# Two attention decodes on one core: B's last two wo rows in four transfers instead of eight, a new order of the last loads, and A's result in one store

## The chip, the cores and the metric

The kernel runs on one core of a Trainium2 chip. The metric is device time in microseconds (us) for one execution. Before the change three runs took 825.72 to 825.73 us, median 825.73 us.

## The reference

Two independent attention decodes, A and B, each with one query token, 32 heads of 128 and its own cache; the two results stand side by side in a [1, 1, 1024] output.

```python
q = (x @ wq)                                   # x: [1, 512], wq: [512, 4096], 32 heads of 128
scores = einsum("bhqd,bhkd->bhqk", q, k) * 128 ** -0.5
p = softmax(scores)
o = einsum("bhqk,bhkd->bhqd", p, v)
result = o.reshape(1, 1, 4096) @ wo            # wo: [4096, 512]
```

A attends to all 16384 keys of each head. B attends to the last 4096 keys. All data are bf16. A's K and V caches (128 MiB each) and the part of B's that is read (32 MiB each) are streamed once through the core; each side's `wq` and `wo` are 4 MiB.

## The kernel before

**The main stream.** The work is cut into 20 steps, 16 of A (two heads each) and 4 of B (eight heads each); step 19, the last, is B's. A step loads an 8 MiB K tile `kt` and an 8 MiB V tile `vt`, all through SyncE's DMA queue (SP), in an order written out by hand (`tc.manual_schedule()`, L382). VectorE (DVE) multiplies K by the query (`scores_prod`, L213) and sums over the head dimension by a tree of adds (`scores_tree`, L219, L223). ScalarE (ACT) makes the exponentials (`soft`), and TensorE (PE) multiplies them by V (`pv`, L277) one step later.

**The tail.** After the last step's scores no K is left to work on, and what remains is short: the last softmax, the last `pv`, the normalisation of both sides, and two products with `wo`:

- `wide_a` (L336): A's output times A's `wo`, 32 matmuls of 512 columns; `finish_a` (L349) adds the four groups of rows, copies the row to SBUF on ACT (L353) and stores it (L355), in three stores on ACT's queue.
- `spread_o(B)` (L325) makes `OpB`, 32 columns of 128 partitions: column r holds the elements 32p + r of B's attention output. A further copy `Ox` (L331) brings the columns 30 and 31 of partitions 64 to 127 down to partitions 0 to 63.
- `project_b` (L357): 30 terms `OpB[:, r]` by `wo_t[:, r, :]`, and two more columns from the tile `extra`, in all one accumulation in a PSUM bank. Each term is four matmuls, one for each quarter of the 512 output columns. Terms 0 to 24 come first, then those of `extra`, then 25 to 29. DVE copies the sum (L374), and four stores, two on SP and two on ACT, write it out (L376).

**Where B's wo lies.** Partition p holds the rows 32p to 32p + 31 of `wo`. Its rows r = 0 to 29 come in four pieces over all 128 partitions, by `load_wo` (L142): piece 0 is rows 0 to 15 (2048 KB), piece 1 rows 16 to 24 (1152 KB), piece 2 rows 25 to 28 (512 KB), piece 3 row 29 (128 KB). The two rows that are left of each partition, 30 and 31 (2 KB together), go by `load_extra` (L147) into 64 partitions of the tile `free`, the lower half of the 128 partitions beside the upper half. This takes eight transfers, written -1 to -8 in the order; each has eight partitions (every fourth one in a group of 32), 4 KB for each partition, 32 KB in all. `wo_order` (L381) is the order in which SP issues them:

```python
wo_order = (-1, -2, -3, 0, -4, -5, -6, 1, -7, -8, 2, 3)
```

**What sets the order.** SP issues its transfers strictly in program order, and waits at the head of its queue. Besides waits for data, the framework gives each transfer one of eight semaphores, in turn, over SP's and ACT's transfers together, in the order in which its planner places them; a transfer waits until the one that had its semaphore before, eight places back, has landed. In the program before, the places at the end are: A's `wo`, -1, -2, -3, piece 0, the three stores of A's row, -4, -5, -6, piece 1, -7, -8, piece 2, piece 3, and the four stores of B's row. A store on ACT's queue can thus hold up a load on SP's. The planner places by its own forecast of time, so where the store of A's row comes among the loads is not written in the kernel.

Of the kernel before, what the change touches and what calls it, by code (L numbers as in the profile page):

```python
# [10 lines left out]
BF16 = mybir.dt.bfloat16  # L11
P = 128
# [4 lines left out]
HQ, DH = 32, 128  # L17
# [8 lines left out]
def kernel(  # L26
# [14 lines left out]
    nc = tc.nc  # L41
# [4 lines left out]
    DN = A_wo.shape[1]  # L46
# [4 lines left out]
    singles = ctx.enter_context(tc.tile_pool(name="singles", bufs=1))  # L51
# [8 lines left out]
    QR = P // NG  # L60

    def kslot(name):
        return kring.tile([P, 2 * CH, DH], BF16, tag="kring", name=name)

    def vslot(name):
        return vring.tile([P, 2 * CH, DH], BF16, tag="vring", name=name)
# [7 lines left out]
    A, B = _Side(), _Side()  # L74
    for k, (s, n, x, wq, wo, nh) in enumerate(((A, "A", A_x, A_wq, A_wo, 2), (B, "B", B_x, B_wq, B_wo, 4))):
# [7 lines left out]
        s.cs = singles.tile([P, HQ // nh], F32, tag=f"cs{n}", name=f"cs{n}")  # L83
        s.mask = singles.tile([P, nh], F32, tag=f"mask{n}", name=f"mask{n}")
        s.acc = ps_o.tile([P, 512], F32, tag=f"acc{n}", name=f"acc{n}")
    Ox = singles.tile([P // 2, 2], BF16, tag="Ox", name="Ox")
    o_banks = [ps_o.tile([P, 512], F32, tag=f"o{k}", name=f"o{k}") for k in range(2)]
    sm_banks = [ps_o.tile([P, 512], F32, tag=f"sm{k}", name=f"sm{k}") for k in range(2)]

# [18 lines left out]
    def flat(t):  # L108
        return t.rearrange("p l d -> p (l d)")
# [15 lines left out]
    def new_k(T):  # L125
        K[T] = kslot("kt")

    def load_k(T, parts=(0, 1)):
        load(T, A_k_cache, B_k_cache, K[T], parts)
# [5 lines left out]
    def load_wq(s):  # L135
        nc.sync.dma_start(  # L136
            out=s.wq_t.rearrange("p (c f) -> p c f", c=KC), in_=s.wq.rearrange("(p c) f -> p c f", c=KC)
        )
# [3 lines left out]
        nc.sync.dma_start(out=s.wo_t[:, r : r + n, :], in_=src[:, r : r + n, :])  # L142

    NX = 2
    PX = P // 2

    def load_extra(s, k):  # L147
        x, b = divmod(k, 4)
        src = s.wo.rearrange("(u p r) f -> p u (r f)", u=2, r=HQ)
        at = slice(32 * x + b, 32 * (x + 1), 4)  # L150
        nc.sync.dma_start(out=extra[at, :, :], in_=src[at, :, (HQ - NX) * DN : HQ * DN])

    def make_masks(s):
# [16 lines left out]
    def clear_x(s, t):  # L170
        s.xb = t[:, 0 : s.nh * KC * P].rearrange("p (h c m) -> p h c m", h=s.nh, c=KC)
        nc.vector.memset(s.xb, 0.0)
# [125 lines left out]
    def pick_blocks(o, src, n, weight):  # L298
        nc.vector.tensor_scalar(out=o, in0=src[:, 0:n], scalar1=weight[:, 0:1], scalar2=None, op0=ALU.mult)
        for j in range(1, 4):  # L300
            nc.vector.scalar_tensor_tensor(
                out=o, in0=src[:, j * n : (j + 1) * n], scalar=weight[:, j : j + 1], in1=o, op0=ALU.mult, op1=ALU.add
            )
# [21 lines left out]
    def spread_o(s):  # L325
        nc.tensor.matmul(s.ps[:, 1 : 1 + P], lhsT=fours[:, :], rhs=s.own[:, :], start=True, stop=True)
        t = small.tile([P, HQ], F32, tag="t", name="t", bufs=1)
        pick_blocks(t[:, :], s.ps[:, 1 : 1 + P], HQ, s.rq)
        nc.vector.tensor_copy(s.Op[:, :], t[:, :])
        if s is B:  # L330
            nc.vector.tensor_copy(Ox[:, :], t[PX:P, HQ - NX : HQ])  # L331

    def o_column(s, r):
        return s.Op[:, r : r + 1].broadcast_to([P, QR])
# [14 lines left out]
    def finish_a():  # L349
        ps = sm_banks[0]  # L350
        nc.tensor.matmul(ps[0:1, :], lhsT=first, rhs=A.wide[:, :], start=True, stop=True)  # L351
        row = one.tile([1, DN], BF16, tag="sc", name="row_a")
        nc.scalar.copy(row[:, :], ps[0:1, :])  # L353
        for a, b in ((0, DN // 2), (DN // 2, 3 * DN // 4), (3 * DN // 4, DN)):
            nc.scalar.dma_start(out=out[0, :, a:b], in_=row[:, a:b])  # L355

    def project_b():  # L357
        w = DN // NG
        ps = sm_banks[1]
        terms = [(o_column(B, r), B.wo_t[:, r, :]) for r in range(HQ - NX)]  # L360
        more = [
            ((Ox[:, j : j + 1] if u else B.Op[0:PX, HQ - NX + j : HQ - NX + j + 1]).broadcast_to([PX, QR]),
             extra[:, u, j * DN : (j + 1) * DN])
            for u in range(2) for j in range(NX)
        ]
        terms = terms[0:25] + more + terms[25:]
        for k, (o, wo) in enumerate(terms):
            for g in range(NG):
                nc.tensor.matmul(  # L369
                    ps[QR * g : QR * (g + 1), 0:w], lhsT=o, rhs=wo[:, g * w : (g + 1) * w],  # L370
                    start=(k == 0), stop=(k == len(terms) - 1),
                )
        rows = one.tile([P, w], BF16, tag="Mr", name="rows_b")
        nc.vector.tensor_copy(rows[:, :], ps[:, 0:w])  # L374
        for g in range(NG):
            (nc.sync if g % 2 else nc.scalar).dma_start(  # L376
                out=out[0, :, DN + g * w : DN + (g + 1) * w], in_=rows[QR * g : QR * g + 1, :]
            )

    wo_pieces = ((0, 16), (16, 9), (25, 4), (29, 1))  # L380
    wo_order = (-1, -2, -3, 0, -4, -5, -6, 1, -7, -8, 2, 3)  # L381
    with tc.manual_schedule():  # L382
        xrow = one.tile([2, D], BF16, tag="pm", name="xrow")
        for s in (B, A):
            nc.scalar.dma_start(out=xrow[s.k : s.k + 1, :], in_=s.x[0, :, :])
        scratch = kslot("scratch")
        new_k(0)
        wqt = vslot("wqt")
        for k, s in enumerate((B, A)):
            s.wq_t = flat(wqt[:, k * CH : (k + 1) * CH, :])  # L390
        load_wq(B)
        load_k(0, (0,))
        load_wq(A)
        load_k(0, (1,))
        make_identity(nc, identf[:, :])
        nc.vector.tensor_copy(two_b[:, :], identf[0:2, 0:2])
        nc.vector.memset(ones[:, :], 1.0)
        nc.vector.tensor_reduce(
            out=quad[:, :], in_=identf[:, :].rearrange("p (m c) -> p c m", c=4), axis=AX.X, op=ALU.add
        )  # L400
        block = small.tile([P, P // 4], F32, tag="block", name="block", bufs=1)
        nc.vector.tensor_reduce(
            out=block[:, :], in_=identf[:, :].rearrange("p (m c) -> p m c", c=4), axis=AX.X, op=ALU.add
        )
        nc.vector.tensor_copy(
            fours[:, :].rearrange("p (m c) -> p m c", c=4), block[:, :].unsqueeze(2).broadcast_to([P, P // 4, 4])
        )
        clear_x(B, flat(scratch[:, :, :]))
        clear_x(A, one.tile([P, 2 * KC * P], BF16, tag="o4", name="xbA")[:, :])
        for o in o_banks:  # L410
            nc.vector.memset(o[:, :], 0.0)
        for s in (B, A):
            make_masks(s)
        turn_x(xrow)
        for s in (B, A):
            spread_x(s)
        project_q(B)
        project_q(A)
        new_k(1)
        load_k(1)  # L420
        for T in range(NT):
            if T >= 1:
                if T + 1 < NT:
                    new_k(T + 1)
                    load_k(T + 1)
                else:
                    load_v(T, kslot("vlast"))
            scores_prod(T, 0)
            if T >= 1:
                max_all(T - 1)  # L430
                soft(T - 1)
            if steps[T][0] is A:
                scores_prod(T, 1)
            else:
                scores_tree(T, 0, CH)
            if T >= 1:
                for u in range(tiles[T - 1].s.units):
                    pv(T - 1, u)
                for u in range(tiles[T - 1].s.units):
                    fold(T - 1, u)  # L440
            if T + 1 < NT:
                load_v(T, vslot("vt"))
            else:
                wot = vslot("wot")
                for k, s in enumerate((A, B)):
                    s.wo_t = flat(wot[:, k * CH : (k + 1) * CH, :]).rearrange("p (r f) -> p r f", r=HQ)
                load_wo(A, 0, HQ)
            if steps[T][0] is A:
                scores_tree(T, 0, 2 * CH)
            else:  # L450
                scores_prod(T, 1)
                scores_tree(T, CH, 2 * CH)
            tile_max(T)
        free = flat(kslot("free")[:, :, :])
        extra = free[0:PX, 0 : 2 * NX * DN].rearrange("p (u n) -> p u n", u=2)
        for k in wo_order:
            if k < 0:
                load_extra(B, -1 - k)
            else:
                load_wo(B, *wo_pieces[k])  # L460
        max_all(NT - 1)
        soft(NT - 1)
        normalize(A)
        own_o(A)
        pv(NT - 1, 0)
        spread_o(A)
        pv(NT - 1, 1)
        normalize(B)
        for u in range(2):
            fold(NT - 1, u)  # L470
        own_o(B)
        wide_a()
        spread_o(B)
        finish_a()
        project_b()


# [28 lines left out]
```

## Time and profile before

| | |
|---|---|
| median of three runs | 825.73 us |
| time of the profiled execution | 825.79 us |
| span of its trace, from the first to the last instruction | 823.7 us |
| busy: DVE, PE, ACT | 755.6, 178.3, 61.4 us |
| read from memory | 352.32 MB, mean 428 GB/s |
| the last K tile's scores end (DVE, L229) | 796.3 us |

Times of the trace count from the start of the span; 2.09 us of the profiled execution's time lie outside it. In a timeline each row has the start, the length from the first instruction's start to the last one's end, the engine, the line, and in brackets the idle time before it and what ended it. "SPq" and "ACTq" are the instructions that issue transfers. A row "wot<-in_B_wo_dram" is a piece of B's `wo`, "free<-in_B_wo_dram" one of the transfers -1 to -8. A transfer's landing shows where an engine that waited for it starts.

### The profile page before, as it was taken

Reading aid. Unit: us, or ns where it says so; the run is one execution under the profiler, and the core shown is the slowest. Engines: PE = TensorE matmul, PEld = TensorE weight load, DVE = VectorE, ACT = ScalarE, POOL = GpSimd, SP = SyncE. Lnnn points to the kernel's source line nnn. Section 1 sums busy time; section 2 is a strip of 40 time slices with the busy share of each in tenths; the row PEclk is TensorE's granted clock in tenths of the full one; section 3 lists DMA queues with packets and bytes.
Section 4 is the critical chain, followed back from the end, with each engine's and each line's share of the span. In section 5 each row is a group of like instructions: output and inputs, shape, how many; then the busy total and the mean of one; then the engine's idle time right before and its main releaser. Section 6 shows DMA issues by size and latency. Waiting matters only on the chain.

```text
span 823.7 us, 3859 instructions
## 1 busy us (share of the span) xinstructions
PE 178.3 (22%) x1614; PEld 59.4 (7%) x1614; DVE 755.6 (92%) x269; ACT 61.4 (7%) x165; POOL 0.7 (0%) x6
## 2 busy tenths in 40 slices
PE   3402212203030302230311213020403020302145
PEld 1100000101010000000000001000100000000012
DVE  2899899999999999999999999998999998999972
ACT  0102000001010000200000001000100000000021
POOL 0000000000000000000000000000000000000000
PEclk9765656566565656555656565565556565656568
DMA  9999999999999999999999999999999999999996
GB/s 384 438 433 437 446 423 446 437 426 439 424 446 423 427 442 442 415 448 426 439 426 437 430 436 421 446 440 420 453 420 446 426 440 426 446 417 450 417 430 252
DMA packets 8146, 352.56 MB, mean 428 GB/s; under 512 B 959, under 2 KB 1090, under 8 KB 1346
## 3 DMA queue, kind: packets, MB, share of 16 engines
q1 hardware_dynamic: 8116, 352.33, 99.1%
q8 instruction: 12, 0.20, 0.1%
q14 instruction: 4, 0.03, 0.0%
q10 hardware_dynamic: 14, 0.00, 0.0%
HBM read 352.32 MB, written 0.00 MB: 428 GB/s over the span
## 4 chain that ended last, share of the span: by engine, by line
DMA 50%; DVE 47%; PE 2%; issue 0%; ACT 0%; SPq 0%; DVEq 0%; ACTq 0%
DMA kt<-in_A_k_cache_dram 44%; DVE kt L213 22%; DVE kt L219 21%; DMA kt<-in_B_k_cache_dram 5%; DVE sc L223 3%; PE o L277 1%; DMA wot<-in_B_wo_dram 0%; DMA out_dram<-row_a 0%; DVE Mr L243 0%; DVE M L239 0%; PE wide L340 0%; PE accB L293 0%; ACT pm L265 0%; PE sm L351 0%; SPq L136 0%
## 5 line engine op out<-in xcount | busy, mean ns | idle before, releaser
L219 DVE TENSOR_TENSOR kt<-kt 128x16384 bf16<-128x16384 bf16 (+3 forms) x96 | 335.1, 3491 | 3.2
L213 DVE TENSOR_TENSOR kt<-kt,qA 128x16384 bf16<-128x16384 bf16 x32 | 277.8, 8682 | 23.3 <-DMA kt<-in_A_k_cache_dram 23.3
L277 PE MATMUL o<-vt,pm 128*8 128x512 bf16 (+1 forms) x1216 | 108.4, 532 | 182.8 <-DMA vt<-in_A_v_cache_dram 163.0
L213 DVE TENSOR_TENSOR kt<-kt,qB 128x16384 bf16<-128x16384 bf16 x8 | 69.5, 8685 | 13.9 <-DMA kt<-in_B_k_cache_dram 13.9
L277 PEld LDWEIGHTS <-pm 128*8 128x8 bf16 (+1 forms) x1280 | 38.5, 111 | 250.2 <-issue 200.8
L233 PE MATMUL sm<-identf,m 128*1 128x128 f32 (+1 forms) x20 | 7.5, 373 | 225.0 <-DVE m L229 225.0
L223 DVE TENSOR_REDUCE sc<-kt 128x256 f32<-128x2048 bf16 (+1 forms) x24 | 46.3, 1931 | 2.1
L246 PE MATMUL sm<-identf,Mr 1*128 1x1 f32 (+1 forms) x20 | 5.2, 262 | 190.1 <-DVE Mr L243 190.1
L252 ACT ACTIVATE bias<-sm 128x1 f32<-128x1 f32 (+1 forms) x20 | 3.4, 171 | 448.7 <-PE sm L246 448.7
L290 ACT COPY o<-o 128x512 f32<-128x512 f32 x24 | 14.1, 586 | 259.1 <-PE o L277 233.0
L293 PE MATMUL accA<-o,foldA 128*32 128x512 f32 x32 | 16.7, 605 | 11.1 <-ACT o L290 11.1
L233 PEld LDWEIGHTS sm<-identf,m 128*1 128x1 f32 (+1 forms) x20 | 1.6, 79 | 242.7 <-DVE m L229 222.5
L246 PEld LDWEIGHTS sm<-identf,Mr 1*128 1x128 f32 (+1 forms) x20 | 3.5, 178 | 196.0 <-DVE Mr L243 196.0
L265 ACT ACTIVATE pm<-p,maskA 128x256 bf16<-128x256 bf16 x32 | 14.5, 501 | 0.5
L190 PE MATMUL qp<-wqt,xbA 128*128 128x512 bf16 x32 | 9.1, 455 | 10.9 <-DMA wqt<-in_A_wq_dram 10.9
L258 ACT ACTIVATE p<-sc,bias 128x256 bf16<-128x256 f32 (+1 forms) x24 | 11.3, 470 | 0.7
L265 ACT ACTIVATE pm<-p,maskB 128x128 bf16<-128x128 bf16 x32 | 10.2, 389 | 0.3
L293 PE MATMUL accB<-o,foldB 128*32 128x512 f32 x16 | 9.6, 694 | 2.0 <-ACT o L290 2.0
L190 PE MATMUL qp<-wqt,scratch 128*128 128x512 bf16 x32 | 8.6, 437 | 4.8 <-DMA wqt<-in_B_wq_dram 4.8
L229 DVE TENSOR_REDUCE m<-sc 128x1 f32<-128x256 f32 (+1 forms) x20 | 8.4, 420 | 0.7
L374 DVE CAST rows_b<-sm 128x128 bf16<-128x128 f32 x1 | 0.3, 292 | 8.6 <-PE sm L369 8.6
L277 PE MATMUL o<-vlast,pm 128*16 128x512 bf16 x64 | 5.8, 530 | 1.6 <-ACT pm L265 1.6
(64 smaller groups left out, 58.5 us busy)
## 6 DMA issues: line engine op xcount, KB each, us to landing
kt<-in_B_k_cache_dram SPq DMA_DIRECT2D x8, 4096.0 KB
vt<-in_B_v_cache_dram SPq DMA_DIRECT2D x6, 4096.0 KB
vlast<-in_B_v_cache_dram SPq DMA_DIRECT2D x2, 4096.0 KB
wqt<-in_B_wq_dram SPq DMA_DIRECT2D x1, 4096.0 KB
wqt<-in_A_wq_dram SPq DMA_DIRECT2D x1, 4096.0 KB
wot<-in_A_wo_dram SPq DMA_DIRECT2D x1, 4096.0 KB
wot<-in_B_wo_dram SPq DMA_DIRECT2D x1, 2048.0 KB
wot<-in_B_wo_dram SPq DMA_DIRECT2D x1, 1152.0 KB
```

The source lines that it names most:

```text
L190: nc.tensor.matmul(qp[:, :, :], lhsT=s.xb[:, j, c, :], rhs=wq[:, c, j, g : g + 4, :], start=(k == 0), stop=(k == n - 1),)
L213: nc.vector.tensor_tensor(out=k, in0=k, in1=s.q[:, j : j + 1, :].broadcast_to([P, CH, DH]), op=ALU.mult)
L219: nc.vector.tensor_tensor(out=k[:, :, 0:w], in0=k[:, :, 0:w], in1=k[:, :, w : 2 * w], op=ALU.add)
L223: nc.vector.tensor_reduce(out=tiles[T].sc[:, lo:hi], in_=k[:, :, 0:8], axis=AX.X, op=ALU.add)
L229: nc.vector.tensor_reduce(out=m[:, 0:U], in_=un.sc[:, :].rearrange("p (u n) -> p u n", u=U), axis=AX.X, op=ALU.max)
L233: nc.tensor.transpose(un.sm[0:U, 0:P], m[:, 0:U], identf[:, :])
L246: nc.tensor.transpose(un.sm[:, P : P + U], Mr[0:U, :], identf[0:U, 0:U])
L258: nc.scalar.activation(out=un.part(p, u), in_=un.part(un.sc, u), func=ACT.Exp, scale=inv, bias=bias[:, u : u + 1], accum_out=s.cs[:, col + ...
L265: nc.scalar.activation(out=un.pm[u][:, :, j, :], in_=un.part(p, u).rearrange("p (i c) -> p i c", c=4), func=ACT.Copy, scale=s.mask[:, j : ...
L277: nc.tensor.matmul(o[r0 : r0 + rows, :], lhsT=un.pm[u][:, i, :, :].rearrange("p a b -> p (a b)"), rhs=V[T][:, u * un.n + 4 * i : u * un.n ...
L290: nc.scalar.copy(osb[:, :], un.o[u][:, :])
L293: nc.tensor.matmul(s.acc[QR * q : QR * (q + 1), :], lhsT=s.fold[:, (per - 1 - off) * rows : (per - 1 - off) * rows + QR], rhs=osb[:, :], s ...
```

## The change

The two rows left over go into 32 partitions, four quarters of the 128 partitions side by side, by four transfers -1 to -4 of eight partitions, 8 KB for each partition, 64 KB in all. `Ox` is made by four copies on DVE, one for each quarter, and the eight terms of `extra` (four quarters by two rows) have 32 rows each, where there were four terms of 64 rows. SP's order becomes -1, piece 0, -2, -3, piece 1, -4, piece 2, piece 3. A's row is stored by one transfer.

```diff
-    Ox = singles.tile([P // 2, 2], BF16, tag="Ox", name="Ox")
+    Ox = singles.tile([P // 4, 4, 2], BF16, tag="Ox", name="Ox")
...
     NX = 2
-    PX = P // 2
-
-    def load_extra(s, k):
-        x, b = divmod(k, 4)
-        src = s.wo.rearrange("(u p r) f -> p u (r f)", u=2, r=HQ)
-        at = slice(32 * x + b, 32 * (x + 1), 4)
+    NU = 4
+    PX = P // NU
+
+    def load_extra(s, b):
+        src = s.wo.rearrange("(u p r) f -> p u (r f)", u=NU, r=HQ)
+        at = slice(b, PX, 4)
         nc.sync.dma_start(out=extra[at, :, :], in_=src[at, :, (HQ - NX) * DN : HQ * DN])
...
         if s is B:
-            nc.vector.tensor_copy(Ox[:, :], t[PX:P, HQ - NX : HQ])
+            for u in range(NU):
+                nc.vector.tensor_copy(Ox[:, u, :], t[PX * u : PX * (u + 1), HQ - NX : HQ])
...
-        for a, b in ((0, DN // 2), (DN // 2, 3 * DN // 4), (3 * DN // 4, DN)):
-            nc.scalar.dma_start(out=out[0, :, a:b], in_=row[:, a:b])
+        nc.scalar.dma_start(out=out[0, :, 0:DN], in_=row[:, :])
...
         more = [
-            ((Ox[:, j : j + 1] if u else B.Op[0:PX, HQ - NX + j : HQ - NX + j + 1]).broadcast_to([PX, QR]),
-             extra[:, u, j * DN : (j + 1) * DN])
-            for u in range(2) for j in range(NX)
+            (Ox[:, u, j : j + 1].broadcast_to([PX, QR]), extra[:, u, j * DN : (j + 1) * DN])
+            for u in range(NU) for j in range(NX)
         ]
...
-    wo_order = (-1, -2, -3, 0, -4, -5, -6, 1, -7, -8, 2, 3)
+    wo_order = (-1, 0, -2, -3, 1, -4, 2, 3)
...
-        extra = free[0:PX, 0 : 2 * NX * DN].rearrange("p (u n) -> p u n", u=2)
+        extra = free[0:PX, 0 : NU * NX * DN].rearrange("p (u n) -> p u n", u=NU)
```

## Prediction

> **What bounds the kernel now.** The page first: what is busy, and how the end is reached.
>
> ```profile
> span 823.7 us, 3859 instructions
> ...
> PE 178.3 (22%) x1614; PEld 59.4 (7%) x1614; DVE 755.6 (92%) x269; ACT 61.4 (7%) x165; POOL 0.7 (0%) x6
> ...
> DMA packets 8146, 352.56 MB, mean 428 GB/s; under 512 B 959, under 2 KB 1090, under 8 KB 1346
> ...
> DMA 50%; DVE 47%; PE 2%; issue 0%; ACT 0%; SPq 0%; DVEq 0%; ACTq 0%
> ```
>
> For most of its span the kernel waits for K or works on it: the stream runs at 428 GB/s, and DVE at 92%. Nothing in the diff is issued before DVE has done with the last K tile, so only the end can change. The chain that ended last, its last pieces (start, us, what):
>
> ```profile
> 785.89 4.43 DVE kt L219
> 799.80 3.59 PE o L277 x16
> 812.80 2.80 DMA out_dram<-row_a
> 816.35 3.80 DMA wot<-in_B_wo_dram
> ```
>
> The end hangs on a load of B's `wo`, and that load on a store of A's row. How can a store hold up a load? The timeline of the last stretch answers it. I pick the rows of SP, of the matmuls that wait for loads, and the last steps.
>
> ```profile
> 795.91 2.31 SPq L151 DMA_DIRECT2D free<-in_B_wo_dram  x3
> ...
> 798.26 0.44 SPq L142 DMA_DIRECT2D wot<-in_B_wo_dram  x1
> ...
> 808.46 2.12 SPq L151 DMA_DIRECT2D free<-in_B_wo_dram  x3
> 808.49 1.42 PEld L340 LDWEIGHTS <-OpA 128*32 128x32 bf16 x32 [0.94 <-DMA wot<-in_A_wo_dram]
> ...
> 810.63 0.43 SPq L142 DMA_DIRECT2D wot<-in_B_wo_dram  x1
> ...
> 812.21 0.17 DVE L331 CAST Ox<-t 64x2 bf16<-64x2 f32 x1
> ...
> 812.80 0.83 ACTq L355 DMA_DIRECT2D out_dram<-row_a  x3
> 813.52 2.78 SPq L151 DMA_DIRECT2D free<-in_B_wo_dram  x2
> 813.55 1.08 PE L369 MATMUL sm<-wot,OpB 128*32 128x128 bf16 x64 [1.39 <-DMA wot<-in_B_wo_dram]
> ...
> 816.35 0.91 SPq L142 DMA_DIRECT2D wot<-in_B_wo_dram  x2
> 816.79 0.69 PE L369 MATMUL sm<-wot,OpB 128*32 128x128 bf16 x36 [2.17 <-DMA wot<-in_B_wo_dram]
> ...
> 817.86 0.29 PE L369 MATMUL sm<-free,OpB 64*32 64x128 bf16 x8 [0.38 <-DMA free<-in_B_wo_dram]
> ...
> 817.98 0.28 PE L369 MATMUL sm<-free,Ox 64*32 64x128 bf16 x8
> ...
> 820.19 0.72 PE L369 MATMUL sm<-wot,OpB 128*32 128x128 bf16 x20 [1.93 <-DMA wot<-in_B_wo_dram]
> ...
> 820.96 0.29 DVE L374 CAST rows_b<-sm 128x128 bf16<-128x128 f32 x1 [8.59 <-PE sm L369]
> ```
>
> Read SP's rows against the landings. -4 goes out at 808.46, when A's `wo` has landed (PE starts on it at 808.49). -7 goes out at 813.52, when piece 0 has landed (PE at 813.55). -8 goes out at the end of its row, 2.78 us long where two issues need less. The waits of SP's queue in this stretch (us in total, times, longest) name all three:
>
> ```profile
> SPq L151 <- DMA wot<-in_A_wo_dram: 9.7, 1, 9.7
> ...
> SPq L151 <- DMA wot<-in_B_wo_dram: 2.4, 1, 2.4
> SPq L151 <- DMA out_dram<-row_a: 1.4, 1, 1.4
> ```
>
> This is the ring of eight semaphores. Count eight places back in the order of the places: from -4 one comes to A's `wo`, from -7 to piece 0, from -8 to the first store of A's row. That store leaves ACT only at 812.80 and lands 2.80 us later, at 815.60; -8, piece 2 and piece 3 stand behind it, and piece 2 is issued at 816.35. By then the data have run out:
>
> ```profile
> 814.00:816.00 2.00, 0.63 (x47) 0.48 (x34) 0.00 (x0) 0.00 (x0) 0.00 (x0) 1.00 0.70 288
> 816.00:818.00 2.00, 0.83 (x48) 0.65 (x51) 0.00 (x0) 0.00 (x0) 0.00 (x0) 1.00 0.37 60
> 818.00:820.00 2.00, 0.26 (x16) 0.18 (x9) 0.00 (x0) 0.00 (x0) 0.00 (x0) 0.62 0.81 290
> ```
>
> The last figure is GB/s: 60 where 428 is usual. **The end is bound by a hole in the stream of loads, and a late issue makes the hole.**
>
> **How large the hole is.** 428 GB/s over 16 DMA engines is 26.75 GB/s for one. I first test that on a stretch without a hole. From piece 0's landing to piece 1's, 813.55 to 816.79, are 3.24 us. In the queue lie between them -4, -5, -6 and piece 1. If a transfer of eight partitions runs on eight engines, each of these carries 3 × 4 KB + 72 KB (of 1024 bytes) = 86,016 bytes: 3.22 us. Spread over sixteen it would be 78 KB, 2.99 us. I take eight engines; the fit says that the stream was unbroken up to piece 1 on the engine that ends last. From piece 1's landing to piece 2's are 820.19 - 816.79 = 3.40 us. Between them lie -7, -8 and piece 2: 2 × 4 + 32 = 40 KB, 40,960 bytes, 1.53 us. The hole is 3.40 - 1.53 = 1.87 us.
>
> **The change, part by part.**
>
> *The transfers and their order.* Eight places back in the new order: A's `wo`, -1, piece 0, -2, -3, piece 1, -4, piece 2, piece 3, with one store somewhere among them. If the store comes before piece 2, piece 2 waits for A's `wo` and piece 3 for -1; if it comes later, piece 3 waits for A's `wo`. Nothing here waits for the store, unless it came ahead of -1. What goes ahead of piece 1 stays equal for each of the eight engines: 3 × 8 KB in place of 6 × 4 KB. So piece 1 still lands for PE at 816.79. Behind it come -4 (8 KB on an engine) and piece 2 (32 KB): 40 KB as before, 1.53 us, now without the hole. PE can start on piece 2 at 816.79 + 1.53 = 818.32 instead of 820.19: **1.87 us less**.
>
> Is the issue early enough? The eight old issues (ns, shortest, median, longest):
>
> ```profile
> L151 SPq DMA_DIRECT2D free<-in_B_wo_dram x8: 666/682/835, 795.9 to 815.6; - x8
> ```
>
> SP is free at 795.91. Four transfers of the new kind and pieces 0 and 1 go before any wait that lasts. A piece costs 0.44 (798.26). A transfer of two rows and eight partitions costs about 0.7 (three in 2.12). One of four rows isn't in the trace: from below 0.44, the row for 128 partitions, from above twice 0.84, the longest of the eight. I take 0.7, by the nearest row. Then SP has issued -4 at 795.91 + 4 × 0.7 + 2 × 0.44 = 799.6, by the upper bound at 803.5; both lie before A's `wo` lands at 808.46. Pieces 2 and 3 follow by about 809.4, when over 7 us of data are still queued. It costs nothing; if the cover were gone, a transfer more would cost its 0.7.
>
> *The bounds of the 1.53.* From A's `wo` to piece 0, 808.49 to 813.55, are 5.06 us for 3 × 4 + 128 = 140 KB, by the rate 5.36: a landing can come 0.3 sooner than the sum, so 1.2 from below. From above, piece 2 has short rows, and 818 to 820 ran at 290 GB/s: 32 KB at 290/16 = 18.1 GB/s are 1.81, with -4's 0.31 2.12 us. I take 1.53, since the 290 holds the start after a hole.
>
> *PE's matmuls.* Terms of `extra` were 16 matmuls with 64 rows and are 32 with 32 rows. The 16 took from 817.86 to 818.26, 0.40 us; the second eight start 0.12 after the first. A matmul of 32 rows isn't shown: from below nothing less than the 0.12 for eight, 0.48 for 32; from above twice the 0.40, 0.80. They start when piece 1's 36 are done, 816.79 + 0.69 = 817.48 (-4's data come 0.31 after piece 1's, before that), and end at 817.96 to 818.28. Piece 2's landing, 818.32, hides them; without that cover they would cost 0.2 to 0.4.
>
> *DVE's copies.* Three more of 0.17 us after 812.38; their reader starts at 817.48. Hidden by 4.5 us; without cover 0.5. `OpB` comes before them, unchanged.
>
> *A's store.* One issue on ACT in place of three (0.83 us); ACT has nothing else to do until B's stores. Nobody waits for it any more. Worth 0 by itself; its worth is in the ring, above.
>
> *The end.* From the start on piece 2 to DVE's copy 0.77 us (820.19 to 820.96), from there to the end of the span 2.74; both stay. **Sum:** 818.32 + 0.77 + 2.74 = 821.83 us of span, 1.87 under 823.7. The profiled execution took 825.79, so 823.92; it lies 0.06 over the median of 825.73. Forecast: **823.9 us**, 0.22% less. A difference of 0.2%, 1.65 us, is about what a measurement of this kernel can tell from no change; the forecast stands only just beyond that, at 824.08.
>
> **The clock of PE** is the term that could move it. The windows about the last matmuls:
>
> ```profile
> 811.65:815.06 3.41, 1.59 (x66) 1.02 (x65) 0.62 (x4) 0.57 (x1) 0.00 (x0) 1.00 0.94 349
> 815.06:818.47 3.41, 1.09 (x52) 0.83 (x52) 0.00 (x0) 0.00 (x0) 0.00 (x0) 1.00 0.44 110
> 818.47:821.88 3.41, 0.72 (x20) 0.45 (x19) 0.29 (x1) 0.00 (x0) 0.00 (x0) 0.50 0.36 138
> ```
>
> The granted clock is full up to 818.47 and half after it, so the last 20 matmuls ran at half. At full clock 64 took 1.08 us and 36 took 0.69: 0.014 for each and 0.19 besides, 0.47 for 20. A clock that stays full gives 0.25 less. After a window with 1.59 us of PE it stayed, after 1.09 it fell. The changed kernel has in the second window 0.69 + (0.48 + 0.28) + 0.15 = 1.60 (the last term from 818.32 to 818.47), as much as the one that stayed; but its matmuls of 32 rows fill a smaller part of the array. I leave it at half for the forecast. The Trainium skill, "TensorE: Matmul & The Clock Gate", Part 1, has the clock go down only after an idle window of about 3.4 us. By that rule it would stay full to the end here, 0.25 us less; the trace speaks against the rule as it stands, since the clock fell after a window with 1.09 us of matmuls.
>
> **The rivals.**
>
> 1. *The clock stays full.* For it the 1.60 us; against it the 32 rows. 823.9 - 0.25 = **823.65**.
> 2. *The store still stands in front of the last pieces* (the change doesn't do what it says): the planner places it so early that pieces 2 and 3 come eight behind it. For it: that is how -8 came to wait. Against it: it would have to stand ahead of A's `wo` (ahead of -1 for piece 3 alone), and it was placed after piece 0. The store lands at 815.60; piece 2 is issued then and not at 816.35, 0.75 sooner: **825.0**, within 0.2%.
> 3. *Piece 2's short rows keep the slow rate* without the hole too: the upper bound, 2.12 for 1.53, **824.5**, within 0.2%.
> 4. *Slower: four rows into one partition.* All of the left-over rows now go to 32 partitions, in groups of four pieces of 2 KB for one partition, where there were two. On each of eight engines these are 16 pieces, by the rate 0.077 us each, 1.22 in all. If the write to one partition becomes their limit, all 1.22 grow by a factor, on the path up to piece 2. It eats the gain at 2.5 times, and is slower by 0.2% at 3.9 times; at five times 823.9 + 4.9 = **828.8**. Against it: with two pieces for a partition the stretch of 3.24 us shows a factor of 1.0.
>
> **How the numbers follow.** Forecast 0.45, rival 1 0.28, rival 2 0.08, rival 3 0.14, rival 4 0.05. Predicted time 823.9. The range reaches down to the lower bound of the 1.53 with the clock at full, in part (1.87 + 0.33 + 0.25 = 2.45, 823.3), and up to cover rival 3 with some of its spread, 824.8; rivals 2 and 4 stay outside. Faster by over 0.2%: rival 1 nearly whole and four fifths of the forecast, 0.27 + 0.37 = 0.64. Slower: rival 4 from 3.9 times, 0.04. The rest, 0.32, is within 0.2%.
>
> **What the changed profile would show.** SP issues all but the last two loads between 795.9 and about 800, and those at about 808.5, with a wait for A's `wo` and none for `row_a`. PE starts on piece 1 at about 816.8 and on piece 2 near 818.3; 816 to 818 shows 200 GB/s or more instead of 60. The chain ends without `out_dram<-row_a`. The forecast is wrong if piece 1 lands later than 816.8 (then rival 4 or an engine that carries more than I count), if SP waits for the store (rival 2), or if the interval from piece 1 to piece 2 is far from 1.5 us.

## The result, and the profile after

The changed kernel takes 823.91 us in the median of 15 runs (822.86 to 824.86), where the kernel before takes 825.73 (825.53 to 826.28): the ratio is 0.9976, with a 95% interval of 0.9969 to 0.9984. That is 1.82 us less. The profiled execution took 824.29 us with a span of 822.3.

The chain that ended last, its end (start, us, what):

```profile
786.07 4.43 DVE kt L219
798.89 17.63 DMA wot<-in_B_wo_dram
816.56 2.80 PE sm L368 x80
```

The store of A's row is gone from it. The chain now runs through piece 1, issued at 798.89, and then through TensorE alone. The timeline of the same stretch as before:

```profile
796.08 0.83 SPq L151 DMA_DIRECT2D free<-in_B_wo_dram  x1
...
796.97 0.39 SPq L142 DMA_DIRECT2D wot<-in_B_wo_dram  x1
...
797.41 1.43 SPq L151 DMA_DIRECT2D free<-in_B_wo_dram  x2
...
798.89 0.44 SPq L142 DMA_DIRECT2D wot<-in_B_wo_dram  x1
...
799.38 0.70 SPq L151 DMA_DIRECT2D free<-in_B_wo_dram  x1
...
808.07 0.80 SPq L142 DMA_DIRECT2D wot<-in_B_wo_dram  x2
...
812.42 0.22 ACTq L355 DMA_DIRECT2D out_dram<-row_a  x1
813.21 1.08 PE L368 MATMUL sm<-wot,OpB 128*32 128x128 bf16 x64 [1.44 <-DMA wot<-in_B_wo_dram]
...
816.56 1.15 PE L368 MATMUL sm<-wot,OpB 128*32 128x128 bf16 x36 [2.27 <-DMA wot<-in_B_wo_dram]
...
817.64 1.04 PE L368 MATMUL sm<-free,Ox 32*32 32x128 bf16 x32
...
818.61 0.72 PE L368 MATMUL sm<-wot,OpB 128*32 128x128 bf16 x20
...
819.38 0.29 DVE L373 CAST rows_b<-sm 128x128 bf16<-128x128 f32 x1 [6.95 <-PE sm L368]
```

All loads but two are issued by 800.1, and pieces 2 and 3 at 808.07, when A's `wo` has landed. Look at the last three rows of matmuls: only the first has a wait in brackets. Piece 2 is in place before TensorE comes to it; from 816.56 on TensorE is never idle. Its windows of the clock say why it takes so long (busy time of PE after the length; the granted clock is the third figure from the end):

```profile
809.67:813.09 3.42, 1.78 (x12) 0.47 (x5) 1.73 (x9) 1.16 (x2) 0.00 (x0) 1.00 0.94 395
813.09:816.50 3.41, 1.08 (x64) 0.93 (x64) 0.00 (x0) 0.00 (x0) 0.00 (x0) 1.00 0.76 305
816.50:819.91 3.41, 2.77 (x88) 2.10 (x87) 0.29 (x1) 0.00 (x0) 0.00 (x0) 0.50 0.07 26
```

The clock fell at 816.50, just as piece 1 landed, and all 88 matmuls behind it ran at half. So 36 of them took 1.15 us where they took 0.69 before. The hole in the loads is closed, and TensorE at half clock is the new bound of this execution. The profiled execution isn't the typical one: at 824.29 us it lies 0.38 above the median.

### The profile page after: what moved, and what is told of

It reads as the page before. It is cut to its first block, busy times and chain, and to the rows that moved or that the text cites. A ratio compares the mean times of both kernels' runs of the same rounds, so it can differ in the third digit from the quotient of the medians.

```text
span 822.3 us, 3888 instructions
## 1 busy us (share of the span) xinstructions
PE 183.8 (22%) x1630; PEld 61.7 (8%) x1630; DVE 756.0 (92%) x272; ACT 61.4 (7%) x165; POOL 0.7 (0%) x6
## 4 chain that ended last, share of the span: by engine, by line
DMA 51%; DVE 47%; SPq 0%; issue 0%; PE 0%; DVEq 0%
DMA kt<-in_A_k_cache_dram 44%; DVE kt L213 22%; DVE kt L219 21%; DMA kt<-in_B_k_cache_dram 5%; DVE sc L223 3%; DMA wot<-in_B_wo_dram 2%; PE sm L368 0%; DVE Mr L243 0%; DVE M L239 0%; SPq L151 0%; SPq L136 0%; DVE m L229 0%; SPq L123 0%; SPq L142 0%; DVE rows_b L373 0%
## 5 line engine op out<-in xcount | busy, mean ns | idle before, releaser
L277 PE MATMUL o<-vt,pm 128*8 128x512 bf16 (+1 forms) x1216 | 113.5, 552 | 182.9 <-DMA vt<-in_A_v_cache_dram 162.6
L239 DVE TENSOR_REDUCE M<-sm 1x2 f32<-1x128 f32 (+1 forms) x20 | 5.4, 272 | 0.5 <-PE sm L233 0.5
```

Source lines behind the costliest of these rows:

```text
L277: nc.tensor.matmul(o[r0 : r0 + rows, :], lhsT=un.pm[u][:, i, :, :].rearrange("p a b -> p (a b)"), rhs=V[T][:, u * un.n + 4 * i : u * un.n ...
```

## The experiments

All kernels were timed in five rounds against the kernel before, which had medians of 825.53 to 825.81 us in these comparisons.

**One store alone.** The kernel before, with one line changed:

```diff
-        for a, b in ((0, DN // 2), (DN // 2, 3 * DN // 4), (3 * DN // 4, DN)):
-            nc.scalar.dma_start(out=out[0, :, a:b], in_=row[:, a:b])
+        nc.scalar.dma_start(out=out[0, :, 0:DN], in_=row[:, :])
```

> The kernel before, with A's row stored by one transfer and nothing else changed. Theory (the ring of eight semaphores: a late store of A's row stands eight places ahead of the last loads and opens the hole): with one store, pieces 2 and 3 come eight places behind piece 0 and the store; piece 2 goes out when piece 0 has landed, about 813.5, and finds the queue full. The hole of 1.87 us closes: 823.7 to 824.1 us where before is 825.7, as much as the whole change. Rival (the four larger transfers and their order bring the gain): nothing changes, 825.7. Rival (both in part): near 824.8.

Measured: 823.82 us, ratio 0.9976 (0.9966 to 0.9985). Eight small transfers in the old order gain as much as the whole change. The timeline of its SP and matmuls:

```profile
809.55 1.41 SPq L151 DMA_DIRECT2D free<-in_B_wo_dram  x2
813.43 1.85 SPq L142 DMA_DIRECT2D wot<-in_B_wo_dram  x2
...
816.82 0.69 PE L368 MATMUL sm<-wot,OpB 128*32 128x128 bf16 x36 [2.29 <-DMA wot<-in_B_wo_dram]
817.43 0.29 PE L368 MATMUL sm<-free,OpB 64*32 64x128 bf16 x8
817.56 0.28 PE L368 MATMUL sm<-free,Ox 64*32 64x128 bf16 x8
818.41 0.72 PE L368 MATMUL sm<-wot,OpB 128*32 128x128 bf16 x20 [0.57 <-DMA wot<-in_B_wo_dram]
```

-7 and -8 go out at 809.55 and piece 2 at 813.43, with piece 0's landing, as counting eight places back says. From its start on piece 1 to its start on piece 2 are now 818.41 - 816.82 = 1.59 us where it was 3.40. The median span is 822.0 where the kernel before has 823.65 in the same comparison, so 1.65 of the 1.9 us lie in the span. The other 0.3 lie outside it, where the places of the ring explain nothing.

**Two stores.** The same, with the row in two halves.

```diff
-        for a, b in ((0, DN // 2), (DN // 2, 3 * DN // 4), (3 * DN // 4, DN)):
+        for a, b in ((0, DN // 2), (DN // 2, DN)):
```

> The kernel before, with A's row in two stores instead of three. Theory (ring): -8 comes eight behind piece 0, piece 2 eight behind the first store, piece 3 behind the second. Piece 2 is issued when the first store lands (815.6) instead of 0.75 us later, so about 0.75 us less than before: 825.0; SP shows a wait for row_a at piece 2. Rival (the number of stores doesn't matter): 825.7.

Measured: 824.58 us (824.03 to 824.79), ratio 0.9985 (0.9976 to 0.9993): between three stores and one, the size of the step missed by 0.4. Piece 2 waits for the store at the place that the count gives (SP's waits in the second block):

```profile
815.41 1.42 SPq L142 DMA_DIRECT2D wot<-in_B_wo_dram  x2
...
818.98 0.74 PE L369 MATMUL sm<-wot,OpB 128*32 128x128 bf16 x20 [2.00 <-DMA wot<-in_B_wo_dram]
```

```profile
SPq L142 <- DMA out_dram<-row_a: 1.6, 1, 1.6
```

TensorE starts on piece 2 at 818.98, 3.57 us after the issue, where it was 820.19 and 3.84 before. Of these 1.21 us, 0.94 are the earlier issue, and the rest a shorter way from issue to landing. Three, two, one store: 825.7, 824.6, 823.8. With SP's waits, which move to where the count of eight puts them, this shows that the places in the ring are the cause of the hole.

**Three stores in the changed kernel.** The converse: the changed kernel, with the old loop of three stores put back.

> The changed kernel with A's row in three stores as before. Theory (ring, places decide, not the store's own cost): piece 2 comes eight behind piece 0, piece 3 eight behind the first store, which still lands by 815.3 with data queued: as the changed kernel, 823.9 within 0.2. Rival (one store instead of three saves the time by itself): 825.5 or more.

Measured: 824.53 us, 823.33 to 825.94, ratio 0.9984 (0.9975 to 0.9993). A miss by 0.6, which neither side had. The spans tell where: their median over the eleven runs is 822.0, the same as that of the changed kernel's fifteen. What lies outside the span is 2.13 us in the median, up to 3.44, against 1.80. In the means, this kernel is 0.75 us over the changed kernel, 0.22 of it in the span and 0.53 outside. So the places cost little or nothing on the path, as the ring has it. In the profiled execution TensorE doesn't wait for piece 2 either, but the clock had fallen even ahead of piece 0's terms:

```profile
813.45 1.79 PE L369 MATMUL sm<-wot,OpB 128*32 128x128 bf16 x64 [1.39 <-DMA wot<-in_B_wo_dram]
```

```profile
810.20:813.61 3.41, 1.70 (x20) 0.64 (x20) 1.73 (x9) 1.16 (x2) 0.00 (x0) 1.00 0.95 396
813.61:817.02 3.41, 1.80 (x73) 1.59 (x68) 0.00 (x0) 0.00 (x0) 0.00 (x0) 0.50 0.77 254
```

**A clock kept up.** The changed kernel with nine matmuls that nobody reads, while TensorE waits for piece 1:

```diff
+        warm = ps_t.tile([P, DN], F32, tag="tp", name="warm")
         for k, (o, wo) in enumerate(terms):
+            if k == 16:
+                for _ in range(9):
+                    nc.tensor.matmul(warm[0:QR, :], lhsT=o_column(A, 0), rhs=A.wo_t[:, 0, :], start=True, stop=True)
```

> The changed kernel with nine matmuls of 512 columns that nobody reads, put on TensorE after piece 0's terms, where it waits for piece 1; about 1.95 us of work, done before piece 1 lands. Theory (the half clock makes TensorE the bound behind piece 1: 1.15 + 0.85 + 0.72 us in the profile of the changed kernel): the clock stays full, TensorE waits for piece 2 again and does the last 20 matmuls in about 0.47 us: 0.5 to 0.8 us less than the changed kernel's profiled 824.3, about 823.4 in the median, with less spread. Rival (the landing of piece 2 bounds in any case): 823.9, no difference. If the nine run past piece 1's landing: later by what they overrun.

Measured: 823.61 us, 823.47 to 824.17 in seven runs, ratio 0.9973 (0.9962 to 0.9984); spans of 821.4 to 821.9 where the changed kernel has 821.1 to 822.6. Its matmuls:

```profile
814.09 2.10 PE L370 MATMUL warm<-wot,OpA 128*32 128x512 bf16 x9
816.60 0.69 PE L372 MATMUL sm<-wot,OpB 128*32 128x128 bf16 x36 [0.41 <-DMA wot<-in_B_wo_dram]
817.22 0.63 PE L372 MATMUL sm<-free,Ox 32*32 32x128 bf16 x32
818.18 0.58 PE L372 MATMUL sm<-wot,OpB 128*32 128x128 bf16 x20 [0.33 <-DMA wot<-in_B_wo_dram]
```

The 36 take 0.69 again, the 32 small ones 0.63, and TensorE waits for piece 2 once more, 818.18 - 816.60 = 1.58 us behind piece 1. Against the profile of the changed kernel the last matmuls start 0.43 sooner. In the median only 0.3 is won, which the two intervals can't tell from nothing. The half clock doesn't come at the same place in every execution: it fell at 816.50 in the profile of the changed kernel, at 817.7 in that with one store alone, and at 813.6, ahead of piece 0's terms, in that with three stores. Outside the span lie 2.03 us here in the median of seven runs, though this kernel has one store, like the changed kernel with its 1.80.

**Three stores with the clock kept up**, to see whether the miss above was the clock:

> The changed kernel with three stores of A's row, as in the run with three stores, which came out at 824.53 where 823.9 was expected, and the nine unread matmuls that keep the clock. Theory (that run's excess was the half clock, which in its profile fell ahead of piece 0's terms; the places of the three stores cost nothing): 823.6 within 0.2, as the changed kernel with the nine matmuls (823.61). Rival (three stores delay the last loads here too): 824.3 or more.

Measured: 824.05 us (823.62 to 825.76), ratio 0.9982 (0.9973 to 0.9991): between the two. The spans have a median of 821.9, 0.2 above that of the nine matmuls with one store; outside lie 2.12 us, up to 3.66, where the kernel with one store has 2.03, up to 2.47. In the means the two are 0.58 apart, 0.21 of it in the span and 0.37 outside. So the clock alone wasn't the cause of the miss. More than half of it is time outside the span, and what sets that time isn't shown.

**Four stores with the clock kept up**, which brings the wait for the store back into the changed kernel:

```diff
-        nc.scalar.dma_start(out=out[0, :, 0:DN], in_=row[:, :])
+        for a, b in ((0, 128), (128, 256), (256, 384), (384, 512)):
+            nc.scalar.dma_start(out=out[0, :, a:b], in_=row[:, a:b])
```

> The changed kernel with the nine unread matmuls and A's row in four stores of 128 columns, so that piece 2 comes eight places behind the first store. Theory (ring): piece 2 goes out when that store lands, about 815.2, and not at 808.1; by the 3.6 us from issue to landing in the run with two stores it lands at 818.8 to 819.0, where 818.14 is in the kernel with one store and nine matmuls: 0.7 to 0.9 later, 824.3 to 824.5; SP shows a wait for row_a at piece 2. Rival (the new transfers close the hole by themselves): 823.6.

Measured: 824.24 us (823.3 to 825.56), ratio 0.9982 (0.9972 to 0.9991). The wait is where it was foreseen:

```profile
814.24 1.73 SPq L142 DMA_DIRECT2D wot<-in_B_wo_dram  x2
...
818.59 0.57 PE L373 MATMUL sm<-wot,OpB 128*32 128x128 bf16 x20 [1.49 <-DMA wot<-in_B_wo_dram]
```

The smaller store landed a microsecond earlier than I had put it, so piece 2 came out only 0.4 late (818.59 against 818.18). The median span is 822.15, 0.45 above that with one store. By its direction the run agrees with the ring. Three stores, without any such wait, cost 0.2 in the span, so that this run weighs little by itself.

**Eight transfers, one store, the clock kept up.** The first kernel with the nine matmuls:

> The kernel before with one store of A's row (823.82) and the nine unread matmuls: eight small transfers, old order, 16 matmuls of 64 rows. Theory (four transfers instead of eight, and 32 matmuls of 32 rows, are worth nothing once the clock is full and the hole closed): 823.6 within 0.2, as the changed kernel with the nine. Rival (fewer transfers save time): 823.9 or more; rival (fewer matmuls save time): 823.2.

Measured: 823.66 us (823.44 to 824.16), ratio 0.9975 (0.9965 to 0.9985). Against 823.61 that is no difference: four transfers instead of eight, the new order and the small matmuls are worth nothing that these runs can tell once the store is out of the way. Its matmuls are divided otherwise, though:

```profile
813.13 1.08 PE L372 MATMUL sm<-wot,OpB 128*32 128x128 bf16 x64 [1.18 <-DMA wot<-in_B_wo_dram]
814.02 2.10 PE L370 MATMUL warm<-wot,OpA 128*32 128x512 bf16 x9
815.87 0.77 PE L372 MATMUL sm<-wot,OpB 128*32 128x128 bf16 x36
...
818.13 0.56 PE L372 MATMUL sm<-wot,OpB 128*32 128x128 bf16 x20 [1.16 <-DMA wot<-in_B_wo_dram]
```

Piece 1 was there by 815.87, 2.74 us behind piece 0 at most, and 2.26 us pass from there to piece 2.

**Even pieces.** If the end hangs on the eight engines that carry the left-over rows, they should be spread over all sixteen. The changed kernel with the nine matmuls and without `extra`:

```diff
-    Ox = singles.tile([P // 4, 4, 2], BF16, tag="Ox", name="Ox")
...
-    wo_pieces = ((0, 16), (16, 9), (25, 4), (29, 1))
-    wo_order = (-1, 0, -2, -3, 1, -4, 2, 3)
+    wo_pieces = ((0, 16), (16, 10), (26, 4), (30, 2))
+    wo_order = (0, 1, 2, 3)
```

> The changed kernel with the nine unread matmuls, and all 32 rows of B's wo in pieces over 128 partitions (16, 10, 4 and 2 rows), no transfers to 32 partitions, no Ox. Each engine then carries 256 KB behind A's wo instead of 272 KB on eight and 240 KB on the others. Theory (the end hangs on the slowest of the eight engines that carry the left-over rows): piece 3 lands 16 KB at 26.75 GB/s, 0.6 us, sooner, PE ends about 0.5 sooner: 823.1. Rival (an engine of the other eight, which now gets 16 KB more, becomes the last): 823.6 or more.

Measured: 825.51 us (825.31 to 825.63), ratio 0.9996 (0.9988 to 1.0005). Both theories missed it: the number lies in the open upper end of the rival, but the loss isn't at the end. TensorE starts on A's `wo` 2.3 us late (808.12 with the nine matmuls alone), while from there to piece 3 everything runs as it should:

```profile
810.40 2.13 PE L337 MATMUL wide<-wot,OpA 128*32 128x512 bf16 x32
...
820.32 0.30 PE L363 MATMUL sm<-wot,OpB 128*32 128x128 bf16 x8 [0.25 <-DMA wot<-in_B_wo_dram]
```

What had changed so far upstream? Leaving out `Ox` had moved the rings of K and V from byte 24576 of a partition to 24544, and with them the small tiles that lie behind the rings. Three runs followed from that.

**Even pieces, `Ox` kept** (the tile and its four copies, which nobody reads):

```diff
+    Ox = singles.tile([P // 4, 4, 2], BF16, tag="Ox", name="Ox")
...
+        if s is B:
+            for u in range(NU):
+                nc.vector.tensor_copy(Ox[:, u, :], t[PX * u : PX * (u + 1), HQ - NX : HQ])
```

> The run with all rows of B's wo over 128 partitions, which came out at 825.51 where 823.1 was expected, again, with the tile Ox and its four copies kept though nobody reads them. Removing Ox had moved the K and V rings from byte 24576 of a partition to 24544. Theory (that shift slowed the main stream: A's wo landed 2.2 us later and K and V loads drifted from the start, while behind A's wo the loads took the 9.9 us that 256 KB at the usual rate take): with the rings back at 24576 A's wo lands at 808.1, piece 3 at about 818.0, and the time is 823.2 within 0.2, 0.4 less than the changed kernel with the nine matmuls (823.61). Rival (even pieces are slower by themselves): 825 or more.

Measured: 823.26 us (822.96 to 823.53), ratio 0.9969 (0.9957 to 0.9981): as expected. Two microseconds hung on 32 bytes of address. Against the 823.61 of the changed kernel with the nine matmuls it is 0.35 less, which the intervals don't tell from no difference.

**The rings moved by 32 and by 64 bytes**, in the changed kernel with the nine matmuls, by a tile ahead of them (16 or 32 elements):

```diff
+    pad = singles.tile([P, 16], BF16, tag="pad", name="pad")
...
+        nc.vector.memset(pad[:, :], 0.0)
```

> The changed kernel with the nine unread matmuls and a tile of 32 bytes for each partition put ahead of the rings, so that they start at 24608 instead of 24576. Theory (a start of the rings that isn't a multiple of 64 bytes slows the stream): 2 us later than with the nine alone, 825.6; A's wo lands near 810. Rival (the even pieces slowed that run, not the address): 823.6.

> The same with a tile of 64 bytes: the rings start at 24640, a multiple of 64 and not of 128. If 64 bytes are the unit that matters: 823.6, as at 24576. If 128 or more: 825.6, as I expect at 24608. If the address doesn't matter: 823.6 in both.

Measured: 826.07 us (825.43 to 826.74) at 24608 and 825.65 us (825.03 to 826.32) at 24640; ratios 1.0004 (0.9995 to 1.0013) and 0.9999 (0.9990 to 1.0008) to the kernel before, 2.5 and 2.0 us above the 823.61 of the same kernel at 24576. A multiple of 64 isn't enough. TensorE starts on A's `wo` at 810.46 and 810.13. At 24576 and at 24608 DVE waits for A's K in all (us, times, longest):

```profile
DVE kt L213 <- DMA kt<-in_A_k_cache_dram: 23.6, 16, 2.6
```

```profile
DVE kt L214 <- DMA kt<-in_A_k_cache_dram: 25.4, 16, 2.7
```

That is 1.8 us more over 16 steps, with the longest wait nearly equal: the stream itself is a little slower all along. In the two traces DVE's multiplications of K start 0.45 us late at 101 us, 1.01 at 449 us and 2.06 at 777 us. Whether the start of the K ring, of the V ring or of a tile behind them does it wasn't separated.

**Even pieces without the nine matmuls.** The kernel with `Ox` kept, and no `warm`:

> The run with even pieces (823.26) without the nine unread matmuls: 64 matmuls stand behind piece 1 instead of 88, and only 8 wait for the last piece. Theory (the clock costs what TensorE has to do behind the landing that it waits for): where the clock has fallen, the last 8 matmuls cost 0.1 to 0.3 more, 823.4 to 823.6 in the median, with more spread than 822.96 to 823.53. Rival (the half clock costs as much here as in the changed kernel, 0.3 in the median and up to 1): 823.6 to 824.2.

Measured: 823.20 us (823.04 to 823.41), ratio 0.9971 (0.9959 to 0.9982), with the 823.26 above the fastest of the study, and with a narrow spread.

```profile
813.24 1.08 PE L363 MATMUL sm<-wot,OpB 128*32 128x128 bf16 x64 [0.91 <-DMA wot<-in_B_wo_dram]
816.28 2.23 PE L363 MATMUL sm<-wot,OpB 128*32 128x128 bf16 x64 [1.96 <-DMA wot<-in_B_wo_dram]
```

Its window from 816 to 818:

```profile
816.00:818.00 2.00, 1.72 (x56) 1.48 (x56) 0.00 (x0) 0.00 (x0) 0.00 (x0) 0.50 0.20 74
```

The clock was at half here too, and no cost of it shows in the median: with 64 matmuls behind piece 1 in place of 88, TensorE is done 2.23 us after piece 1's landing, not 2.8. Neither expectation has the clock cost as little as this. The best version found is the plainest: all rows of `wo` over 128 partitions, one store, no helper transfers.

## Why the prediction was right, and where it was lucky

**The hole and its cause: right, and shown.** SP issues the last loads without waiting for the store, and one store alone does the same for the kernel before. The stores' number sets the gain in steps (825.7, 824.6, 823.8), with nothing else changed. Of the gain in the median, 1.65 us lie in the span, where the hole was. Rival 2, a store still in the way, didn't come true; when it was brought about with four stores, the wait came back, and the span grew by 0.45, of which 0.2 came with three stores already.

**The 1.53 us from piece 1 to piece 2: right in size, but not fixed.** It is 1.58 and 1.59 us in two kernels above in which TensorE waits for piece 2, and 2.26 in the one with eight transfers, one store and the nine matmuls, where piece 1 came sooner (815.87). What stays equal is the whole way from the start on piece 0 to the start on piece 2: 4.95, 4.98 and 5.00 us in these three, where the prediction has 3.24 + 1.53 = 4.77. Piece 1 came 2.84 us behind piece 0 with two stores, and at most 2.74 with eight transfers and one store, less even than the 2.99 of sixteen engines. So the fit of the 3.24 us on eight engines was in part luck, and how many engines carry such a transfer stays open. Rival 3 (2.12 us) isn't needed for the 4.95 to 5.00. Rival 4 falls: with four pieces for one partition the whole way is the same as with two.

**Piece 1 at 816.79:** 816.56, 0.23 sooner.

**"The landing of piece 2 hides the matmuls": this step failed in the profiled execution.** I had put the 36 and the 32 matmuls at full clock, to end at 817.96 to 818.28, and only the last 20 at half. I carried the windows of the clock over from the profile of before, where one ends at 818.47. In the changed kernel one ends at 816.50, and after 1.08 us of matmuls in it the clock fell. From piece 1 to the start on piece 2 are 2.05 us in place of 1.53. The nine unread matmuls confirm it: with the clock up, TensorE waits for the landing again. Rival 1 looked at the right mechanism from the wrong side: the clock moved, and against the kernel. Its place in an execution isn't fixed. That part of the spread of 822.86 to 824.86 follows from it is likely but not shown: with the nine matmuls the spans spread over 0.5 us in seven runs instead of 1.5 in fifteen, but over 1.2 with four stores, and over 0.3 with even pieces and the clock at half.

**"From there to the end of the span 2.74; both stay", and 2.09 outside it: neither stayed.** In the profiled execution 2.92 us lie between DVE's copy and the end of the span, 0.18 more. Outside the span are 1.80 us in the median of the changed kernel's runs, against 2.09 in the kernel before. The kernel before with one, two and three stores has 1.81, 1.93 and 2.09 there, as if the stores set it. But one store has 2.03 in the changed kernel with the nine matmuls, and 2.01 and 2.03 in the two runs with moved rings, and four stores have 1.95. What the time is made of stays open.

So the sum came out because its errors cancel. The profiled span of 822.3 is 0.47 over the 821.83 of the sum: 0.23 less by piece 1, 0.52 more from piece 1 to the start on piece 2 (2.05 for 1.53), and 0.18 more at the end. In medians the span fell by 1.65 (823.65, over the 28 runs beside the first four kernels, to 822.0) where 1.87 was forecast, and 0.3 came from outside the span, which I hadn't in the sum. The forecast sign, its cause and about the size of the hole stand; 823.9 to the tenth was luck.

**What the profile would show:** the waits of the loads and the chain came as said. SP does show one wait for `row_a` (7.0 us), but at the last stores, ahead of which it has nothing to do. "816 to 818 shows 200 GB/s or more" didn't: it is

```profile
812.00:814.00 2.00, 0.79 (x57) 0.79 (x60) 0.37 (x3) 0.39 (x1) 0.00 (x0) 1.00 0.99 413
...
816.00:818.00 2.00, 1.44 (x52) 1.24 (x55) 0.00 (x0) 0.00 (x0) 0.00 (x0) 0.62 0.18 70
```

The engines were busy for 0.18 of that stretch in the mean, and the data had gone earlier (413 GB/s from 812 to 814, where it was 338). The figure is a mean over all engines; which of them ends last, and when, this view doesn't show.

## What to carry to other kernels

A transfer can wait for another one with which it shares neither data nor queue, only a semaphore: where the chain shows a store ahead of a load, count the places back in the ring before redesigning the loads, for one line may do what a new layout does. When a wait for data goes, work out what the engine behind it needs at half clock, since it idled just before. Keep an eye on where the big rings start: an edit that removes a 32-byte tile can cost more than the edit gains.

## What the runs showed of the hardware

- The start of the K and V rings, and of the tiles behind them, matters: at byte 24576 of a partition the same kernel takes 823.61 us, at 24608 826.07 and at 24640 825.65; with the even pieces 823.26 at 24576 and 825.51 at 24544. Which multiple is needed, and for which tile, wasn't tried beyond that.
- TensorE's clock fell after a window of 3.41 us with 1.08 us of matmuls here, after one with 1.09 in the kernel before, and stayed after 1.59 there. The busy time of a window alone doesn't settle it: in the run with three stores the clock fell after one with 1.70 us, from 810.20 to 813.61, and in the kernel before it stayed after less. By the Trainium skill, "TensorE: Matmul & The Clock Gate", Part 1, an idle window is what lowers it; these rows, with matmuls in the window, differ from that, and the measurement decides. The same part calls the window free-running, which does not reset when a kernel starts; with that the trace agrees: one begins at 815.06 in the kernel before and at 813.09 in the changed one, counted from the start of the span.
